# Attention two batches ahead of the output layer, with two float32 batches, in an attention and feed-forward kernel

## The chip, the core and the metric

The kernel runs on one core of a Trainium2 chip. The metric is device time in microseconds of one launch, as a median of several runs. Its engines: TensorE (PE) multiplies matrices and writes the accumulator (PSUM), VectorE (DVE) and ScalarE (ACT) work on elements, GpSimd (POOL) does small work in SBUF, and SyncE (SP) issues the transfers (DMA). Each engine takes its own instructions in order; semaphores order them against each other.

## The reference

```python
scores = (q @ k.T) / sqrt(64) - log(448)          # q, k, v: 8 batches, 12 heads, 448 x 64, float32
attn = 1 / (1 + exp(-scores))                     # a sigmoid, no sum over the row
x = (attn @ v) -> (8 * 448) x 768                 # heads side by side
h = x @ w_in                                      # 768 x 2048
g = where(h > 0, h, exp(min(h, 0)) - 1)           # ELU
out = g @ w_out                                   # 2048 x 768, float32
```

The weights w_in and w_out come as 64-bit floats, the rest as float32.

## The kernel before

**Precision.** A value in float32 is split into a high and a low float16 half (`split`, L120 to L122: ScalarE writes the high half, VectorE the low one), and a product is three matmuls: high x high, low x high, high x low. Scales that are powers of two keep the halves in range. They come from maxima: `magnitude` (L98) multiplies a diagonal by the row maxima (tile `dg`, VectorE), lets TensorE spread it over the partitions (`pb`) and reduces it on VectorE (`al`, then `pw`). Batches below `EXACT` are treated differently: their queries, keys and values stay float32 and go to TensorE as such, each product one float32 matmul instruction or two, so that they need no halves and almost no scales.

**Stages.** A batch has six pairs of heads. For a pair, `prepare` (L294) works in three steps, which callers can place apart: the maxima and `dg`; the scales (`pb`, `al`, `pw`, `sc`, on TensorE, VectorE and GpSimd); and `transposed` (L331), which for a float32 batch transposes queries and keys on TensorE into the accumulator (tile `pt`) and copies them out to `early`, and for the others makes the halves `nat` and transposes them by DMA to `qk` (L352), and makes the halves `vn` of the values. Then a `Pair` computes `scores` (L384, tile `psc`, two buffers) for four groups of keys (three of 128 for both heads, one with the last 64 of each), `soften` (the sigmoid at L395, and for float16 batches the halves `at` at L413 and L414), `values` (L425, L433, tile `pav`, one buffer) and `finish` (`split` to `xh`, and its maximum). Two buffers of `xh` hold the attention of two batches.

After six pairs `rescale` (L443) brings the pairs of a batch to one scale, `moe1` (L479) computes the hidden layer `g` in 16 blocks of 18 matmuls with their exponentials (`ph` at L499, `e` at L511 to L514, `split` to `g`), and `moe2` (L558) computes the output in tiles of 48 matmuls (`po`, L529), which come in 16 steps of three. An even batch has six such tiles (96 steps); an odd one eight (128 steps), as the last 64 tokens of both batches share a tile for each half of the columns.

**Before the loop.** Batch 0 is float32. Beside its pairs, w_in is loaded in 16 tiles (768 KB each) to `stage`, turned from 64-bit floats to magnitudes and signs (`magnitudes`, `signed`, L132 to L159) and split to `wi`; the list `W_IN` says how many tiles are done behind each pair. Then batch 0's hidden layer is computed, and beside it w_out is treated, by a generator of 64 steps (`load_w_out`, L202): for each half of the columns 16 steps that load and turn a block, and 16 that split one. `w_out_beside` makes four steps (`W_OUT`) for each block of the hidden layer from the third on. w_out's tile `wo` shares its place with `stage`. This part is put in order by a planner, which takes the program's order as priority and issues what is ready by its own model of the times.

**The loop** (from L686) runs over batches 1 to 7, and there the order of TensorE, ScalarE, VectorE and SyncE is the program's. Round b mixes the attention of batch b with the output of batch b - 1, then computes the hidden layer of b:

```python
for t in range(2): p.scores(t); p.soften(t)
third()                                  # halves and DMA transpose for the next pair
# loads for the third pair ahead
fill(gap)                                # output steps of three matmuls
second = prepare_pair(n + 2)             # maxima and dg
for t in range(2, NC + 1): p.scores(t); p.soften(t)
fill(share - gap - tail)
third = second()                         # pb, al, scales
for t in range(NC + 1): p.values(t)
p.finish(); fill(tail)                   # tail: four steps in the last pair, 0 in the others
```

In the last pair the generator `hidden` has been started (`next(h)`, the rescaling) ahead of the second `fill`; the second `next(h)` behind the six pairs computes the hidden layer. ScalarE keeps the sigmoid and the exponential in different tables; an order is added so that it changes table once each way for a batch (L398). Lines of the groups below that many parts share: L121 and L122 are `split`, L125 is `absmax`, L105 to L114 are `magnitude`.

## Time and profile before

| | |
|---|---|
| median of 3 runs | 1272.22 us (1271.79 to 1273.72) |
| the profiled execution | 1270.86 us |
| its span | 1269.1 us |
| TensorE busy | 1200.2 us, 95% |
| VectorE busy | 823.4 us, 65% |
| ScalarE busy | 671.8 us, 53% |
| GpSimd busy | 84.1 us, 7% |
| mean granted clock of TensorE | 0.984 |

The profile has one execution. Its span is the time from the first to the last instruction; busy time of TensorE is modelled for the ends of its matmuls, so that back-to-back matmuls overlap a little and the distance of their starts is the better price. A group of instructions is listed by line, engine, operation and tile, with the count, busy time, mean duration of one in ns, and the idle time of its engine just before them with what ended it. The chain of waits is followed back from the last instruction.

### The profile page before, as it was taken

What the parts mean: (1) busy time and instruction counts of PE and PEld (TensorE: products, weight loads), DVE (VectorE), ACT (ScalarE), POOL (GpSimd) and SP (SyncE); (2) the same over time, 40 slices, a digit from 0 to 9 for tenths busy, and PEclk for the clock granted to TensorE, in tenths of its full rate; (3) what the DMA queues carried; (4) which work ended last, traced back from release to release, by engine and by line L of the source; (5) the groups of instructions that cost most, each with busy time, mean ns of one, the idle gap of its engine ahead of it and who ended that gap; (6) DMA issues with size and microseconds to landing.
All of it is one profiled execution on the core that took longest, in us unless ns stands there. A gap on an engine that the chain in (4) does not pass through costs nothing.

```text
span 1269.1 us, 19337 instructions
## 1 busy us (share of the span) xinstructions
PE 1200.2 (95%) x7246; PEld 610.5 (48%) x7246; DVE 823.4 (65%) x1872; ACT 671.8 (53%) x1015; POOL 84.1 (7%) x319
## 2 busy tenths in 40 slices
PE   5979868999999999999999999999999999999998
PEld 2324334445555554545455554545455554455565
DVE  5898989765766557775666646885576656765500
ACT  5867777643655337744555436654565435663400
POOL 0011001100000000010000000010000100100000
PEclk9889979999999999999999999999999999999999
DMA  8937423420233103340144201440034401410000
GB/s 229 281 100 222 126 77 80 100 49 1 60 84 89 37 1 83 89 86 1 37 92 92 50 1 43 105 103 7 1 86 92 92 1 22 106 43 7 1 25 26
DMA packets 213407, 89.76 MB, mean 71 GB/s; under 512 B 177472, under 2 KB 209216, under 8 KB 213312
## 3 DMA queue, kind: packets, MB, share of 16 engines
q1 hardware_dynamic: 213312, 88.51, 28.7%
q8 instruction: 57, 0.93, 0.3%
q14 instruction: 38, 0.31, 0.1%
HBM read 58.20 MB, written 11.01 MB: 55 GB/s over the span
## 4 chain that ended last, share of the span: by engine, by line
PE 78%; ACT 8%; DVE 7%; DMA 3%; issue 2%; SPq 2%; DVEq 0%; POOL 0%; ACTq 0%; POOLq 0%
PE ph L499 31%; PE po L529 25%; PE psc L384 7%; PE pav L433 6%; PE po_r L529 5%; PE pav L425 3%; ACT sg L395 2%; DMA stage<-in_moe_w_in_dram 2%; ACT at L413 1%; SPq L262 1%; PE pb L110 1%; ACT L395 1%; ACT e L511 1%; DVE e L514 1%; DMA so<-in_moe_w_out_dram 1%
## 5 line engine op out<-in xcount | busy, mean ns | idle before, releaser
L499 PE MATMUL ph<-xh,wi 128*128 128x448 f16 x2304 | 442.0, 353 | 6.1 <-DVE xh L122 2.4
L529 PE MATMUL po<-wo,g 128*128 128x384 f16 x2304 | 392.9, 328 | 0.0
L529 PEld LDWEIGHTS <-g 128*128 128x128 f16 x2688 | 257.2, 98 | 198.4 <-issue 36.3
L499 PEld LDWEIGHTS <-wi 128*128 128x128 f16 x2304 | 225.3, 98 | 218.4 <-issue 7.6
L511 ACT ACTIVATE e<-ph,msc 128x448 f32<-128x448 f32 x128 | 80.8, 633 | 211.7 <-PE ph L499 211.6
L414 DVE SCALAR_TENSOR_TENSOR at<-sg,at 128x896 f16<-128x896 f32 x126 | 137.2, 1090 | 84.5 <-ACT at L413 84.5
L395 ACT ACTIVATE sg<-psc,bias,sc 128x896 f32<-128x896 f32 (+1 forms) x168 | 166.6, 992 | 1.7
L513 DVE TENSOR_SCALAR e<-e 128x448 f32<-128x448 f32 x128 | 50.3, 394 | 170.8 <-ACT e L511 170.7
L121 ACT ACTIVATE xh<-pav,sc 128x448 f16<-128x448 f32 x48 | 30.3, 632 | 216.7 <-PE pav L425 216.7
L384 PE MATMUL psc<-qk 64*128 64x448 f16 x1008 | 116.6, 355 | 11.4 <-ACT sg L395 11.4
L413 ACT ACTIVATE at<-sg 128x896 f16<-128x896 f32 x126 | 119.8, 951 | 4.1
L121 ACT ACTIVATE g<-e,msc 128x384 f16<-128x384 f32 (+1 forms) x192 | 96.0, 534 | 6.0 <-DVE e L514 4.3
L122 DVE SCALAR_TENSOR_TENSOR g<-e,msc,g 128x384 f16<-128x384 f32 (+1 forms) x192 | 94.6, 521 | 0.6
L514 DVE SCALAR_TENSOR_TENSOR e<-ph,msc,e 128x448 f32<-128x448 f32 x128 | 87.3, 683 | 4.0
L384 PEld LDWEIGHTS <-qk 64*128 64x128 f16 x1008 | 41.7, 97 | 89.7 <-issue 60.2
L433 PE MATMUL pav<-at,vn 128*64 128x448 f16 x756 | 80.2, 357 | 0.0
L324 POOL TENSOR_SCALAR sc<-pw 128x1 f32<-128x1 f32 x42 | 12.4, 295 | 843.5 <-DVE pw L114 790.9
L529 PE MATMUL po_r<-wo,g 128*128 128x384 f16 x384 | 64.7, 326 | 0.0
L122 DVE SCALAR_TENSOR_TENSOR xh<-pav,sc,xh 128x448 f16<-128x448 f32 x48 | 32.7, 680 | 48.7 <-ACT xh L121 48.7
L433 PEld LDWEIGHTS <-vn 128*64 128x64 f16 x756 | 39.4, 110 | 50.0 <-issue 27.8
L122 DVE SCALAR_TENSOR_TENSOR nat<-raw,sc,nat 128x384 f16<-128x384 f32 (+1 forms) x126 | 59.1, 524 | 0.0
L121 ACT ACTIVATE nat<-raw,sc 128x384 f16<-128x384 f32 (+1 forms) x126 | 58.8, 529 | 0.0
(103 smaller groups left out, 852.7 us busy)
## 6 DMA issues: line engine op xcount, KB each, us to landing
stage<-in_moe_w_in_dram SPq DMA_DIRECT2D x16, 768.0 KB, 6.6
raw<-in_q_dram SPq DMA_DIRECT2D x96, 96.0 KB, 3.1
raw<-in_k_dram SPq DMA_DIRECT2D x96, 96.0 KB, 2.6
rv<-in_v_dram SPq DMA_DIRECT2D x48, 192.0 KB, 2.7
out_dram<-o SPq DMA_DIRECT2D x48, 192.0 KB, 2.1
wo<-in_moe_w_out_dram SPq DMA_DIRECT2D x19, 384.0 KB, 4.1
so<-in_moe_w_out_dram SPq DMA_DIRECT2D x13, 384.0 KB, 4.3
raw<-in_q_dram SPq DMA_DIRECT2D x48, 32.0 KB, 2.4
```

The source lines that it names most:

```text
L121: nc.scalar.mul(hi, src, s)
L122: nc.vector.scalar_tensor_tensor(lo, src, s, hi, op0=ALU.mult, op1=ALU.subtract)
L384: nc.tensor.matmul(psc[:, j, :S] if g < NC else psc[rows[j], 0, :S], kk[rows[j], o], qq[rows[j], :S], start=(n == 0), stop=(n == len(parts ...
L395: a = nc.scalar.activation(sg[:, :nb], psc[:, :nb, :S], AF.Sigmoid, bias=bias, scale=self.s_scale)
L413: nc.scalar.mul(hi, sg, 2.0**ATOP)
L414: nc.vector.scalar_tensor_tensor(lo, sg, 2.0**ATOP, hi, op0=ALU.mult, op1=ALU.subtract)
L433: nc.tensor.matmul(pav[rows[j], :S], vv[i][:, j * NC + g], sg[k][:, j], start=(g == 0 and n == 0), stop=False,)
L499: nc.tensor.matmul(ph[:, :S], wi[:, wj, c, f * P : (f + 1) * P], xh[:, c, xj], start=(n == 0), stop=(n == 3 * NK - 1),)
L511: a = nc.scalar.activation(e, ph[:, :S], AF.Exp, scale=inv)
L513: nc.vector.tensor_scalar(e, e, 1.0, -1.0, op0=ALU.min, op1=ALU.add)
L514: nc.vector.scalar_tensor_tensor(e, ph[:, :S], inv, e, op0=ALU.mult, op1=ALU.max)
L529: nc.tensor.matmul(po[:, :HM], lh(gj, f), wo[:, i, f, wj], start=(n == 0), stop=(n == 3 * NF - 1),)
```

## The change

`EXACT` becomes 2, so batch 1 is computed in float32 too, ahead of the loop. The loop runs over batches 2 to 7; round b mixes the attention of b with the output of b - 2, and then computes the hidden layer of b - 1. Behind the loop come the output of batch 6, the hidden layer of batch 7 and the output of batch 7. The rescaling is cut in five, one piece for each of the first five pairs, and the four reserved steps (`tail`) go. w_in's tiles are spread a little differently over batch 0's pairs. w_out's treatment begins behind the seventh pair: five steps behind each of the pairs 7 to 12, two for each block of batch 0's hidden layer, and the rest in the loop. `prepare_pair(n + 2)` moves behind the last scores of a pair, and its scales (`second()`) move from ahead of the values to behind the next pair's first two groups of scores, straight before the halves; the first pair of a round takes 10 output steps there and no longer 8. In a float32 pair ScalarE copies one half of the transposed queries and keys from the accumulator and VectorE the other. The exponentials of batch 0 are ordered behind the last sigmoid of batch 1, and `xs` has a third buffer.

```diff
-    EXACT = 1
+    EXACT = 2
-    W_IN = [1, 3, 6, 9, 12, 15, 16]
+    W_IN = [1, 3, 6, 9, 12, 14, 16, 16, 16, 16, 16, 16, 16]
+    W_OUT_FROM = 6
-    W_OUT = 4
+    W_OUT, W_OUT_PAIR = 2, 5
...
-                nc.vector.tensor_copy(qk, pt[:, : 2 * S])
+                nc.scalar.copy(qk[:, :S], pt[:, :S])
+                nc.vector.tensor_copy(qk[:, S:], pt[:, S : 2 * S])
...
-            if b - 1 in last_exp:
+            last_sigmoid[b] = a.ins.name
+            if b - EXACT in last_exp:
                 tc.add_manual_dep(
                     a.ins,
-                    last_exp[b - 1],
+                    last_exp[b - EXACT],
...
         for c in range(NP - 1):
             nc.vector.tensor_scalar(xh[:, c], xh[:, c], rr[:, c : c + 1], None, op0=ALU.mult)
+            yield
...
+            if b == 0:
+                tc.add_manual_dep(
+                    a.ins,
+                    last_sigmoid[EXACT - 1],
...
-            xs_of[b] = sb.tile([P, 3, NP], F32, tag="xs", name=f"xs{b}", bufs=2)
+            xs_of[b] = sb.tile([P, 3, NP], F32, tag="xs", name=f"xs{b}", bufs=3)
...
+    def w_out_begin():
+        nonlocal wo, steps
+        w_in_ratios()
+        wo = sb.tile([P, NH, NF, 2, HM], F16, tag="wo", name="wo")
+        steps = load_w_out(wo)
+
     def w_out_beside(f):
-        if f >= 2:
-            step(W_OUT)
-        if f == NF - 1:
-            step(1)
+        step(W_OUT)
...
+        if n == W_OUT_FROM:
+            w_out_begin()
+        if n >= W_OUT_FROM:
+            step(W_OUT_PAIR)
-    third = prepare_pair(EXACT * NP + 1)()
+    second = prepare_pair(EXACT * NP + 1)
...
-            tiles = moe2(b - 1, g, wo)
-            left = NF * NH * (NC + (b - 1) % 2)
+            tiles = moe2(b - 2, g, wo)
+            left = NF * NH * (NC + b % 2)
...
-                tail = 4 if hp == NP - 1 else 0
...
-                third()
+                second()()
...
-                gap = 8 if hp == 0 else 5
+                gap = 10 if hp == 0 else 5
                 fill(gap)
-                second = prepare_pair(n + 2)
                 for t in range(2, NC + 1):
                     p.scores(t)
                     p.soften(t)
+                second = prepare_pair(n + 2)
...
-                if hp == NP - 1:
-                    h = hidden(b)
+                if hp == 0:
+                    h = hidden(b - 1)
+                if hp < NP - 1:
                     next(h)
-                fill(share - gap - tail)
-                third = second()
+                fill(share - gap)
                 for t in range(NC + 1):
                     p.values(t)
                 p.finish()
-                fill(tail)
...
-        out_scale(*of_moe2)
-        for _ in moe2(B - 1, g, wo):
-            pass
+        for b in range(B - 2, B):
+            out_scale(*of_moe2)
+            if b < B - 1:
+                h = hidden(b + 1)
+                for _ in range(NP - 1):
+                    next(h)
+            for _ in moe2(b, g, wo):
+                pass
+            if b < B - 1:
+                of_moe2 = next(h)
```

More of the change, by code (lines that the diff above doesn't have):

```diff
@@ L240, in load_w_out @@
                 yield
-    last_exp = {}
+    last_exp, last_sigmoid = {}, {}
     def load_keys(dst, rest, src, b, h0):
@@ L453, in rescale @@
         )
-        yield
         mx, xp, xr = (rr[:, NP + i : NP + i + 1] for i in range(3))
@@ L512, in moe1 @@
             last_exp[b] = a.ins.name
+            if b == 0:
+                tc.add_manual_dep(
+                    a.ins,
+                    last_sigmoid[EXACT - 1],
+                    mybir.DependencyInfo(
+                        mybir.DependencyClass.NoSync, mybir.DependencyReason.DATA
+                    ),
+                    reason="one change of tables",
+                )
             nc.vector.tensor_scalar(e, e, 1.0, -1.0, op0=ALU.min, op1=ALU.add)
@@ L614, in prepare_pair @@
         return second
-    def w_out_beside(f):
-        nonlocal wo, steps
-        if f == 0:
-            w_in_ratios()
-            wo = sb.tile([P, NH, NF, 2, HM], F16, tag="wo", name="wo")
-            steps = load_w_out(wo)
-        if f >= 2:
-            step(W_OUT)
-        if f == NF - 1:
-            step(1)
+    def w_out_begin():
[3 more added lines that the diff above has]
+        steps = load_w_out(wo)
+    def w_out_beside(f):
+        step(W_OUT)
     def pair_of(n):
@@ L634, in hidden @@
         whole = rescale(b, xh, xs)
-        next(whole)
-        yield
+        for _ in range(NP - 1):
+            next(whole)
+            yield
         xp, xr, rest = next(whole)
@@ L678, in attention_ffn @@
     h = hidden(0, w_out_beside)
-    next(h)
+    for _ in range(NP - 1):
+        next(h)
     of_moe2 = next(h)
@@ L729, in attention_ffn @@
             of_moe2 = next(h)
-        out_scale(*of_moe2)
-        for _ in moe2(B - 1, g, wo):
-            pass
+        for b in range(B - 2, B):
+            out_scale(*of_moe2)
+            if b < B - 1:
+                h = hidden(b + 1)
+                for _ in range(NP - 1):
+                    next(h)
+            for _ in moe2(b, g, wo):
+                pass
+            if b < B - 1:
+                of_moe2 = next(h)
 _INS = ["q", "k", "v", "moe_w_in", "moe_w_out"]
```

## The prediction

> **What bounds the kernel now.** I read the page first, then the chain of waits in order of time, then windows cut at the stages that the chain shows.
>
> ```profile
> span 1269.1 us, 19337 instructions
> PE   5979868999999999999999999999999999999998
> ```
>
> From the sixth slice on TensorE is at 9 tenths nearly everywhere; only the first five slices (159 us) and slice 40 have room. The chain gives the length of a batch, because every run of 270 hidden matmuls is one piece of it:
>
> ```profile
> 269.27 51.09 PE ph L499 x270
> ...
> 421.99 51.09 PE ph L499 x270
> ...
> 563.55 51.09 PE ph L499 x270
> ...
> 716.27 51.09 PE ph L499 x270
> ...
> 1151.20 51.08 PE ph L499 x270
> 1202.28 23.40 PE po L529 x144
> 1225.68 7.80 PE po_r L529 x48
> ...
> 1256.88 7.81 PE po_r L529 x48
> ```
>
> A loop round with 128 output steps (the output of an odd batch) takes 421.99 - 269.27 = 152.72 us, one with 96 steps 563.55 - 421.99 = 141.56. Of these, 51.09 are the run itself, so from the end of a run to the next run's start a 96-step round takes 90.47. A hidden matmul costs 51.09/270 = 0.189 us, an output matmul 23.40/144 = 0.1625.
>
> Going back 90.47 from 269.27, the kernel stands as if the hidden layer of batch 0 had ended, with nothing left over, at **178.8 us**. That early stretch is where the change works:
>
> ```profile
> 30.00:87.00 57.00, 47.56 (x232) 17.54 (x233) 51.01 (x130) 46.27 (x60) 4.83 (x13) 0.88 0.75 219
> 87.00:103.00 16.00, 12.86 (x76) 6.68 (x75) 15.14 (x50) 7.81 (x11) 4.95 (x14) 1.00 0.07 17
> 103.00:162.40 59.40, 52.60 (x269) 25.47 (x268) 54.72 (x121) 46.05 (x94) 2.84 (x9) 0.97 0.60 185
> 162.40:178.80 16.40, 6.87 (x38) 3.11 (x36) 10.88 (x22) 11.29 (x20) 0.00 (x0) 0.77 0.31 96
> ```
>
> Columns: stretch, length, busy time of TensorE, its weight loads, VectorE, ScalarE, GpSimd, then granted clock, DMA share and GB/s. To 103 us the float32 pairs and w_in keep VectorE at 89 to 95%; to 162.4 the hidden layer of batch 0 and w_out keep it at 92%; then TensorE starves (6.87 of 16.40) while w_out is finished. Before 178.8 VectorE is the bound, behind it TensorE.
>
> **The change, part by part.**
>
> *A batch moves from float16 three times to float32 twice.* What one float32 pair costs TensorE is read from start to start in a stretch without gaps:
>
> ```profile
> 58.91 0.97 PE L384 MATMUL psc<-early 64*64 64x448 f32 x4
> 59.81 0.97 PE L433 MATMUL pav<-sg,rv 128*64 128x448 f32 x4
> 60.72 0.98 PE L337 MATMUL pt<-ident,raw 128*128 128x128 f32 x7
> 61.54 0.92 PE L425 MATMUL pav<-sg,rv 128*128 128x448 f32 x2
> 62.38 1.02 PE L384 MATMUL psc<-early 64*128 64x448 f32 x4
> ```
>
> A scores group takes 0.90, a values group 0.91, the seven transposes 0.82, the rest of the values 0.84: 4 x 0.90 + 3 x 0.91 + 0.82 + 0.84 = 8.0 us a pair, 48 for six. What the batch cost in the loop is read from a 96-step round:
>
> ```profile
> 473.08:563.55 90.47, 85.56 (x578) 43.00 (x579) 68.25 (x156) 57.03 (x76) 8.95 (x37) 1.00 0.42 91
> ```
>
> 90.47 less 288 output matmuls (46.8) and the first 18 hidden ones (3.4) leaves 40.3, of which TensorE stood 90.47 - 85.56 = 4.9: 35.4 of work. So TensorE has 12.6 us more to do, and the change can pay only by filling idle time.
>
> *The early stretch anew.* From 87 us TensorE has 48 (six pairs), 288 x 0.189 = 54.5 (hidden layer of batch 0), 32 sums of w_out at 0.1625 = 5.2 and about 1 for the maxima: **109 us**. VectorE has the rows above, 15.14 + 54.72 + 10.88 = 80.7, and for each new pair:
>
> ```profile
> L125 DVE TENSOR_REDUCE mx<-rv 128x1 f32<-128x512 f32 x48 | 32.6, 679 | 0.6 <-DMA rv<-in_v_dram 0.5 <-issue 0.2
> ...
> L122 DVE SCALAR_TENSOR_TENSOR xh<-pav,sc,xh 128x448 f16<-128x448 f32 x48 | 32.7, 680 | 48.7 <-ACT xh L121 48.7
> ...
> L125 DVE TENSOR_REDUCE xs<-xh 128x1 f32<-128x448 f16 x48 | 29.2, 609 | 0.0
> ...
> L341 DVE COPY early<-pt 128x896 f32<-128x896 f32 x6 | 6.5, 1090 | 8.2 <-PE pt L337 8.0
> ...
> L122 DVE SCALAR_TENSOR_TENSOR wo<-wo,swo 128x384 f16<-128x384 f32 x28 | 16.4, 613 | 2.6 <-ACT wo L121 2.3
> ...
> L395 ACT ACTIVATE sg<-psc,bias 128x896 f32<-128x896 f32 (+1 forms) x24 | 21.0, 906 | 2.1 <-PE psc L384 2.1
> ```
>
> 0.68 + 0.68 + 0.61 + half of 1.09 + some 0.5 of small ones = 3.0, six times 18; about 10 more splits of w_out before the loop (the steps left over at 178.8) 6; less half a copy for each of the first six pairs, 3.3: 101 us. ScalarE: 7.81 + 46.05 + 11.29 = 65, four sigmoids a pair (21.0/6 = 3.5), the split of xh and the new half copy at about 0.6 each (estimate, from the 0.68 and half of 1.09 on VectorE): 28, splits 6, three or four for the first six pairs: 102. TensorE is the longest. How closely it can be filled is the one number that I choose: 1.00 as the upper bound, 47.56/57 = 0.83 (the first six pairs beside w_in) as the lower. 103 to 162.4 gave 52.60/59.40 = 0.89 with VectorE as the bound; here w_out's steps lie beside 109 us of matmuls, not beside 60, and VectorE needs 101 of the time, so I take 0.90: 121 us, so the hidden layer of batch 0 ends at **208 us** (196 to 218), against 178.8.
>
> The stretch from 162.4 had the clock at 0.77 while TensorE stood. [...]
>
> *Attention two batches ahead.* Hidden layer b-1 no longer waits for the last pair of b, so its four reserved output steps go back before the values. The wait that this shortage of cover made goes too:
>
> ```profile
> PE pb L110 <- DVE dg L105: 11.6, 6, 2.0
> ...
> ACT xh L121 <- PE pav L425: 216.7, 41, 7.4
> ```
>
> ```profile
> 486.75 0.32 PE L110 MATMUL pb<-dg,ones 128*128 128x384 bf16 x1 [1.97 <-DVE dg L105]
> ...
> 555.05 0.32 PE L110 MATMUL pb<-dg,ones 128*128 128x384 bf16 x1 [1.91 <-DVE dg L105]
> ```
>
> Six such waits of 1.9 us: one in the first and one in the last pair of each of three 96-step rounds. Those of the last pairs go: 1.9 in each. In the first pair the wait for dg goes, but the chain below takes its place, and the gap of 10 steps for 8 only moves filling from one wait to the other: zero for both. The five rescalings (0.45 each) now lie one to a pair beside output matmuls; their cover is a VectorE that is 75% busy there (68.25 of 90.47); without it each would delay the pair by its 0.45.
>
> *Scales move behind the next pair's first scores.* This is the edit that can cost. Now they are ready when ScalarE reaches the split of nat:
>
> ```profile
> 508.17 1.40 ACT L121 ACTIVATE nat<-raw,sc 128x384 f16<-128x384 f32 x3
> 508.30 1.09 DVE L414 SCALAR_TENSOR_TENSOR at<-sg,at 128x896 f16<-128x896 f32 x1 [0.88 <-ACT at L413]
> ...
> 510.78 1.54 SPq L352 DMA_TRANSPOSE qk<-nat  x1
> 511.09 0.95 ACT L413 ACTIVATE at<-sg 128x896 f16<-128x896 f32 x1
> ...
> 514.32 1.89 PE L433 MATMUL pav<-at,vn 128*64 128x448 f16 x18
> ...
> 515.46 0.55 DVE L112 TENSOR_REDUCE al<-pb 128x3 f32<-128x384 f32 x1
> ...
> 516.93 0.23 POOL L319 TENSOR_SCALAR sc<-sc 128x3 f32<-128x3 f32 x1
> ...
> 517.09 1.12 PE L384 MATMUL psc<-qk 64*128 64x448 f16 x10
> ```
>
> and of the transposes of all pairs
>
> ```profile
> DMA to landing us min/median/max: 3.9/4.0/5.5
> ```
>
> After the change al stands behind the second low half (ends 509.39), and al to the scales takes 517.16 - 515.46 = 1.7, so nat begins near 511.1, not 508.17: 2.9 later. Behind nat on ScalarE stand the split of vn and the last two sigmoids, and for them wait the values: the third high half ends at 512.04 + 2.9 = 515.0, its low half 1.09 later at 516.1, where the last two values want it at about 515.9. VectorE's part of nat ends some 2.6 later, so the transpose is issued at 513.4 and lands 4.0 later at 517.4, where the next scores started at 517.09. So the pair grows by about **0.3 us**. On SP the loads of the third pair ahead stand behind the waiting transpose, with two pairs to spare. Bounds: 0 (it is all within the slack) and 1.0 (VectorE's work for a pair and its waits for POOL and ScalarE in a row). In a 128-step round the pair has over 2 us more output matmuls, and the cost is zero. Three 96-step rounds x (5 x 0.3 + 0.2 for the first pair) = 5 us (0 to 15).
>
> *Nothing:* the third xs buffer, the other split of w_in's tiles, the added order behind the last sigmoid (the exponentials wait for the last pair's values anyway).
>
> **The sum.** To the next run of hidden matmuls: 208 + 90.47 - 1.9 = 296.6. Then three rounds of 152.72 and two of 139.66: 737.5. Then the run itself 51.09, the output of batch 6 46.8, the hidden layer of batch 7 54.5, the output of batch 7 23.40 + 7.80 + 23.40 + 7.81 = 62.4, and the 4.4 from 1264.69 to the end: 219.2. With the 5 of the scales: **1258.3 us** of span. The profiled execution took 1270.86 for its span of 1269.1, and the median is 1272.22; with these 3.1 I say **1261 us**.
>
> **The rivals.**
>
> *Slower: the second float32 batch keeps the pace of the first.* Place: pairs 7 to 12.
>
> ```profile
> L425 PE MATMUL pav<-sg,rv x12: 539/540/643, 25.3 to 87.0; 128*128 128x448 f32 x12
> ```
>
> Six pairs from 25.3 to 87.0 are 12.3 us a pair, though TensorE needs 8.0: ScalarE, VectorE and TensorE pass one pair back and forth, with w_in's tiles queued in between. For it: w_out's five steps a pair (each about 1.1 us of VectorE and of ScalarE while it loads, 0.6 while it splits) queue in the same places. Against: in that stretch w_in also kept the DMA engines at 0.75. Price: 6 x 12.3 = 74, then 57 us of hidden layer and sums at 0.89, 64: 225, and 1278 us. It decides from (221 - 87 - 64)/6 = 11.7 us a pair, where the sum passes 1274.8.
>
> *No change: the chain of the scales costs its upper bound.* 15 pairs x 1.0 in place of 5: 1271 us. For it: VectorE's queue in a pair, whose order is now fixed through two other engines. Against: ScalarE stood idle 216.7 us in 41 waits for the values before the split of xh (the row above), 5.3 each, more than the 2.9 that is added.
>
> *Faster still: TensorE is filled throughout.* It ends at 196 to 198, 1250 us. Against: VectorE would be over 92% busy.
>
> **How the numbers follow.** Forecast 0.50 (1254 to 1269, which is the early stretch ending at 201 to 216), filled throughout 0.12, scales 0.14, slow pairs 0.24. A change within 0.2% (2.5 us) can't be told from none here. Faster 0.62, same 0.15, slower 0.23. The range reaches from the filled stage to the slow pairs: 1249 to 1279.
>
> **What would show it.** The hidden layer of batch 0 ends near 208 us; the run of 270 matmuls that follows the first loop round starts near 297; rounds of 152.7 and about 141. Waits of TensorE for dg at the ends of batches are gone. Wrong if the float32 pairs after 87 us are over 11.7 us apart, or if the 96-step rounds are over 144 us.

## The result and the profile after

The changed kernel takes a median of 1287.76 us (1287.18 to 1288.71), the kernel before 1272.15 us in the same runs: the ratio is 1.0121 (95% interval 1.0103 to 1.0139). The change makes it 1.2% slower. The forecast was 1261 us in a range of 1249 to 1279, so the sign is wrong and the time lies outside the range.

The page of the changed kernel begins as follows (span, then TensorE's busy tenths and the granted clock in 40 slices of 32 us):

```profile
span 1285.8 us, 19086 instructions
PE   5778899899999999999999999999999999999998
PEclk9879999999999999999999999999999999999999
```

Slice 6 (159 to 190 us), in which TensorE starved before, is full now (9 for 6), as forecast; a smaller hole, slice 8, lies behind the hidden layer of batch 0 in its new place. But slice 2 is emptier than before (7 for 9), and the clock is at 8 and 7 tenths in slices 2 and 3, which is the first float32 batch.

Next the chain of waits in order of time (start, length, engine, work). Each run of 270 hidden matmuls ends a stage, as before:

```profile
321.66 51.09 PE ph L502 x270
...
474.60 51.09 PE ph L502 x270
...
617.76 51.09 PE ph L502 x270
...
770.69 51.09 PE ph L502 x270
...
913.69 51.09 PE ph L502 x270
...
1066.48 51.08 PE ph L502 x270
```

And windows of the changed kernel, cut where the last values of the sixth and of the twelfth float32 pair start and where the hidden layer of batch 0 ends (stretch, length, busy time of TensorE, weight loads, VectorE, ScalarE, GpSimd, clock, DMA share, GB/s):

```profile
30.00:60.00 30.00, 19.97 (x108) 7.73 (x108) 21.11 (x53) 23.27 (x33) 0.92 (x5) 0.94 0.91 268
60.00:100.40 40.40, 33.25 (x151) 12.13 (x152) 31.98 (x81) 27.58 (x35) 2.90 (x11) 0.75 0.47 123
100.40:168.60 68.20, 57.97 (x251) 18.48 (x250) 54.59 (x150) 55.14 (x95) 5.41 (x18) 0.97 0.54 162
168.60:227.10 58.50, 56.80 (x303) 28.51 (x302) 45.39 (x96) 33.34 (x62) 3.44 (x9) 1.00 0.33 95
```

The forecast, stage by stage, against these rows:

| stage | forecast, us | measured, us |
|---|---|---|
| sixth float32 pair | 87 (as before, 86.6) | 100.4 |
| from there to the end of batch 0's hidden layer | 121 | 227.1 - 100.4 = 126.7 |
| from there to the next run of 270 | 88.6 and 1.7 for the scales | 321.66 - 227.1 = 94.6 |
| 128-step rounds | 152.72 | 152.94, 152.93, 152.79 |
| 96-step rounds | 139.66 and 1.7 | 143.16, 143.00 |
| the rest | 219.2 | 1285.8 - 1066.48 = 219.3 |

The span is 27.5 us over the forecast's 1258.3. The first batch brings 13.4 of it, the second batch and the hidden layer 5.7, the first round 4.3, the two 96-step rounds 3.4; the remaining 0.7 is spread over the rest. So 19 of 27.5 us were lost before the loop begins, and half of the whole in the first batch, in which the change touches only the copy in halves and the place of one tile of w_in.

### The profile page after: what moved, and what is told of

The parts are those of the page before. It is cut to its first block, busy times and chain, and to the rows that moved or that the text cites. A ratio compares the mean times of both kernels' runs of the same rounds, so it can differ in the third digit from the quotient of the medians.

```text
span 1285.8 us, 19086 instructions
## 1 busy us (share of the span) xinstructions
PE 1221.2 (95%) x7204; PEld 616.5 (48%) x7204; DVE 789.9 (61%) x1794; ACT 648.3 (50%) x983; POOL 85.0 (7%) x289
## 4 chain that ended last, share of the span: by engine, by line
PE 65%; ACT 13%; DVE 11%; DMA 5%; issue 4%; SPq 1%; POOL 0%; DVEq 0%; ACTq 0%; POOLq 0%
PE ph L502 30%; PE po L541 19%; PE po_r L541 5%; ACT sg L397 4%; PE psc L386 4%; PE pav L436 4%; ACT at L416 3%; DMA stage<-in_moe_w_in_dram 2%; PE pav L428 2%; DVE at L417 2%; DVE mt L126 1%; ACT nat L122 1%; DMA so<-in_moe_w_out_dram 1%; DVE wo L123 1%; DVE mx L126 1%
## 5 line engine op out<-in xcount | busy, mean ns | idle before, releaser
L541 PE MATMUL po<-wo,g 128*128 128x384 f16 x2304 | 387.0, 326 | 0.4 <-DVE e L526 0.4
L417 DVE SCALAR_TENSOR_TENSOR at<-sg,at 128x896 f16<-128x896 f32 x108 | 117.8, 1091 | 90.7 <-ACT at L416 90.3
L397 ACT ACTIVATE sg<-psc,bias,sc 128x896 f32<-128x896 f32 (+1 forms) x144 | 142.7, 991 | 2.9 <-PE psc L386 1.2
L416 ACT ACTIVATE at<-sg 128x896 f16<-128x896 f32 x108 | 102.6, 950 | 3.4
L386 PE MATMUL psc<-qk 64*128 64x448 f16 (+1 forms) x864 | 100.2, 356 | 1.4 <-ACT sg L397 0.8
L122 ACT ACTIVATE nat<-raw,sc 128x384 f16<-128x384 f32 (+1 forms) x108 | 50.9, 533 | 100.2 <-POOL sc L320 100.2
L123 DVE SCALAR_TENSOR_TENSOR g<-e,msc,g 128x384 f16<-128x384 f32 (+1 forms) x192 | 94.6, 521 | 2.8 <-ACT g L122 2.4
L436 PE MATMUL pav<-at,vn 128*64 128x448 f16 x648 | 73.5, 358 | 14.3 <-ACT at L416 10.7
L549 DVE TENSOR_SCALAR o<-po,osc 128x384 f32<-128x384 f32 x48 | 29.4, 613 | 78.8 <-PE po L541 71.6
L386 PEld LDWEIGHTS <-qk 64*128 64x128 f16 (+1 forms) x864 | 35.4, 98 | 70.0 <-issue 39.7
L386 PE MATMUL psc<-early 64*128 64x448 f32 (+1 forms) x192 | 54.4, 651 | 7.2 <-DVE early L343 2.9
```

Source lines behind the costliest of these rows:

```text
L122: nc.scalar.mul(hi, src, s)
L123: nc.vector.scalar_tensor_tensor(lo, src, s, hi, op0=ALU.mult, op1=ALU.subtract)
L386: nc.tensor.matmul(psc[:, j, :S] if g < NC else psc[rows[j], 0, :S], kk[rows[j], o], qq[rows[j], :S], start=(n == 0), stop=(n == len(parts ...
L397: a = nc.scalar.activation(sg[:, :nb], psc[:, :nb, :S], AF.Sigmoid, bias=bias, scale=self.s_scale)
L416: nc.scalar.mul(hi, sg, 2.0**ATOP)
L417: nc.vector.scalar_tensor_tensor(lo, sg, 2.0**ATOP, hi, op0=ALU.mult, op1=ALU.subtract)
```

## The experiments

All stage times come from the traces: "sixth" and "twelfth" are the starts of the last values matmuls of those float32 pairs, "hidden 0" is the start of the last matmul of batch 0's hidden layer, "round" is the first 96-step round between two runs of 270. The "first round" in the text goes from the end of batch 0's hidden layer to the end of the next run of 270. The ratio is against the kernel before.

A trace is one execution. In the six kernels with one copy on VectorE (those named with one_copy) the traces have the same order of instructions on every engine up to the sixth pair, and yet it stands anywhere between 86.2 and 90.9 us. So a difference of less than 5 us in that column is not shown by two traces.

| kernel | sixth | twelfth | hidden 0 | round | median, us | ratio (95%) |
|---|---|---|---|---|---|---|
| before | 86.6 | - | 161.8 | 141.6 | 1272.2 | 1 |
| after | 100.4 | 168.6 | 226.9 | 143.2 | 1287.8 | 1.0121 (1.0103 to 1.0139) |
| after_one_copy | 90.4 | 158.9 | 218.1 | 143.3 | 1276.8 | 1.0027 (1.0011 to 1.0042) |
| before_two_copies | 99.8 | - | 170.2 | 141.5 | 1279.5 | 1.0044 (1.0031 to 1.0058) |
| after_copies_vector | 94.1 | 159.4 | 216.9 | 144.4 | 1279.0 | 1.0045 (1.0031 to 1.006) |
| after_copy_scalar | 90.8 | 155.8 | 212.6 | 143.3 | 1273.6 | 1.0005 (0.9992 to 1.0019) |
| before_copy_scalar | 88.6 | - | 168.2 | 141.5 | 1275.0 | 1.0015 (1.0001 to 1.0028) |
| after_w_in | 100.6 | 175.3 | 233.1 | 143.6 | 1294.3 | 1.0161 (1.0144 to 1.0178) |
| after_scales | 99.4 | 173.3 | 236.2 | 141.2 | 1288.8 | 1.0119 (1.0098 to 1.014) |
| before_moved_scales | 85.9 | - | 164.4 | 146.8 | 1291.6 | 1.0149 (1.0128 to 1.0171) |
| one_copy_scales | 86.4 | 155.8 | 221.0 | 141.2 | 1274.2 | 1.0016 (0.9999 to 1.0032) |
| one_copy_scales_w33 | 86.2 | 153.7 | 218.3 | 141.2 | 1273.1 | 1.0009 (0.9995 to 1.0024) |
| one_copy_late | 86.4 | 147.4 | 216.5 | 143.7 | 1285.6 | 1.011 (1.0092 to 1.0129) |
| one_copy_scales_loop | 90.9 | 158.5 | 217.1 | 141.2 | 1269.6 | 0.9982 (0.9969 to 0.9995) |
| one_copy_scales_loop_w62 | 89.4 | 157.4 | 218.4 | 141.2 | 1268.0 | 0.9973 (0.9958 to 0.9988) |
| copy_scalar_scales | 90.8 | 156.9 | 214.6 | 141.1 | 1268.3 | 0.996 (0.9947 to 0.9973) |
| copy_scalar_scales_w62 | 90.2 | 154.6 | 213.3 | 141.3 | 1267.4 | 0.9953 (0.9936 to 0.997) |

### The copy in halves

**The changed kernel with one copy.**

```diff
-                nc.scalar.copy(qk[:, :S], pt[:, :S])
-                nc.vector.tensor_copy(qk[:, S:], pt[:, S : 2 * S])
+                nc.vector.tensor_copy(qk, pt[:, : 2 * S])
```

> The changed kernel with one edit undone: VectorE alone copies queries and keys out of the accumulator. In the changed kernel the first six float32 pairs end at 100.4 us instead of 86.6 (the start of the last values matmul of the sixth pair), and the stage before the loop ends at 227 instead of the 208 forecast. Theory A (the half copy on ScalarE holds them up, since scores now wait for whichever of two queues is later): the sixth pair is back near 87 to 90 us and the kernel 10 to 14 us shorter, about 1275. Theory B (the copy is not the cause; twelve float32 pairs and w_out put the planned part in another order): within 4 us of 1287.8, sixth pair near 100.

Measured: the sixth pair at 90.4 instead of 100.4, 11.0 us of the median gone.

**The kernel before with two copies**: the same edit the other way round.

> The kernel before with that one edit alone: one half of queries and keys copied by ScalarE, the other by VectorE. Theory A: the sixth float32 pair comes 8 to 14 us later than 86.6 us, and the kernel takes about 1280 us. Theory B: within 3 us of 1272.2.

Measured: the sixth pair at 99.8 instead of 86.6. The hidden layer of batch 0 takes back a part (it ends 8.4 us later), and the median is 6.8 us above the 1272.7 of the kernel before in the same runs. This edit, for which no wait was costed, is worth 7 us here and 11 there. In the four traces with halves in two queues (after, before_two_copies, after_w_in and after_scales) the sixth pair stands at 99.4 to 100.6 us, in the twelve with a whole copy at 85.9 to 90.9.

How it works is seen in the timeline of before with two copies, at the end of its second pair (start, length, engine, line, instruction):

```profile
41.00 0.98 PE L337 MATMUL pt<-ident,raw 128*128 128x128 f32 x7
...
42.04 0.56 ACT L341 COPY early<-pt 128x448 f32<-128x448 f32 x1
...
43.03 0.95 DVE L157 SCALAR_TENSOR_TENSOR stage<-stage 128x768 uint32<-128x768 uint32 x1
...
43.46 1.02 PE L385 MATMUL psc<-early 64*128 64x448 f32 x4
...
43.90 0.62 DVE L342 COPY early<-pt 128x448 f32<-128x448 f32 x1
...
44.86 1.02 PE L385 MATMUL psc<-early 64*128 64x448 f32 x4
```

The transposes are done near 42.0 and ScalarE's half starts at once, at 42.04. VectorE's half starts at 43.90: ahead of it in VectorE's queue stands a 0.95 us instruction for a tile of w_in. The next scores, at 43.46, start before that half does. They don't read it: a pair is transposed ahead of the scores of the pair before it, so the transposes are the fourth pair's and the scores the third's. What the scores need is room in the accumulator. `pt`, which the transposes write, is one of the two buffers of `psc` (`tag="psc", bufs=2` in the kernel), and it comes free when both halves are copied out. The first group of scores takes the other buffer; the second starts at 44.86, 0.34 us behind the end of VectorE's half (43.90 + 0.62 = 44.52).

It is so throughout. In the changed kernel's trace the first group behind the transposes starts before the last copy ends in eleven of twelve pairs; the second never does, and in eight pairs it starts within 0.25 us of that end. So the later of two queues sets when the scores go on, and w_in's tiles stand in both. From the end of the transposes to the end of the last copy it is, as a mean of the first six pairs, 3.2 us here and 1.2 in the kernel before; 3.6 in the changed kernel, 1.4 with one copy on VectorE, 1.7 with one on ScalarE and 1.6 with both halves on VectorE.

What TensorE waited for in the first batch, from 20 us to the sixth pair's end, for the kernel before:

```profile
PE pav L433 <- ACT sg L395: 7.1, 3, 3.6
PE psc L384 <- ACT sg L395: 2.9, 4, 1.5
20.00:87.50 67.50, 54.25 (x274) 20.58 (x273) 61.31 (x158) 54.69 (x71) 5.61 (x18) 0.90 0.80 226
```

for before with two copies:

```profile
PE pav L434 <- ACT sg L396: 15.7, 6, 4.9
20.00:100.80 80.80, 59.01 (x290) 22.90 (x287) 64.64 (x165) 59.17 (x79) 5.87 (x18) 0.85 0.69 190
```

(waited for: total, times, longest; the last row is the window). TensorE's idle time rises from 67.50 - 54.25 = 13.3 us to 21.8. The wait that grows is for the sigmoid, which is late because its scores are late; the scores themselves hardly show a wait for a copy, since TensorE is given other work there. That is 8.5 of the 13.3 us by which this stretch is longer. The rest is slower work: TensorE is busy 4.8 us longer, for 16 instructions more, at a clock of 0.85 instead of 0.90. Windows in the loop, below, show the clock at 0.50 behind some waits.

**Which property of the halves it is.** In one kernel both halves are on VectorE, in another one whole copy is on ScalarE:

```diff
-                nc.scalar.copy(qk[:, :S], pt[:, :S])
+                nc.vector.tensor_copy(qk[:, :S], pt[:, :S])
```

> The changed kernel with both half copies on VectorE, as two instructions. Theory A1 (ScalarE is the cause: in the first batch its queue holds w_in's work, and its half of the copy comes late): the sixth pair is near 87 to 91 us as with one copy, and the kernel takes 1274 to 1280. Theory A2 (two instructions instead of one change the planner's order, whichever engine runs them): the sixth pair near 100, about 1287.

```diff
-                nc.scalar.copy(qk[:, :S], pt[:, :S])
-                nc.vector.tensor_copy(qk[:, S:], pt[:, S : 2 * S])
+                nc.scalar.copy(qk, pt[:, : 2 * S])
```

> The changed kernel with the whole copy on ScalarE, as one instruction. Theory A1: the sixth pair near 100 us or later, 1285 to 1295. Theory A2: near 87 to 91 us and about 1277. Theory A3 (what hurts is that the scores wait for the later of two queues): like A2, since there is one queue again.

Measured: 94.1 us with two halves in one queue, 90.8 with one copy on ScalarE, 90.4 with one on VectorE, 100.4 with halves in both queues. The theory that ScalarE's queue is the wrong place fell: the whole copy on ScalarE gives the lowest median of the four, 1273.6 us, though its interval overlaps that of one copy on VectorE; VectorE is relieved of 12 x 1.09 = 13 us there, and the second batch takes 65.0 us instead of the 68.5 with one copy on VectorE. Two queues instead of one are worth 8.8 us of the median (1287.8 for 1279.0) with the same two instructions. Whether two instructions in one queue cost anything is not shown: the medians are 2.2 us apart (1279.0 and 1276.8) and the intervals overlap. On ScalarE the whole copy takes 0.90 us, from the groups of that kernel:

```profile
L342 ACT COPY early<-pt 128x896 f32<-128x896 f32 x12 | 10.8, 900 | 5.7 <-PE pt L338 5.7
```

**The kernel before with its copy on ScalarE**: the same edit.

> The kernel before with the whole copy of queries and keys moved to ScalarE. Theory A3 (it is the split over two queues that costs): the sixth pair within 4 us of 86.6 and the kernel within 4 us of 1272.6, where the two halves on two engines cost 7 us. Theory A2 in its strict form (any change of the copy reorders the early stretch for the worse): 1276 or more. If ScalarE is simply the better place for it: 1265 to 1269.

Measured: 1.0015 (1.0001 to 1.0028), 2.3 us slower by the medians. So in the kernel before, with six float32 pairs, the copy on ScalarE brings nothing.

### The scales behind the next pair's scores

**The kernel before with the scales moved**, alone:

```diff
-    third = prepare_pair(EXACT * NP + 1)()
+    second = prepare_pair(EXACT * NP + 1)
...
-                third()
+                second()()
...
-                second = prepare_pair(n + 2)
                 for t in range(2, NC + 1):
                     p.scores(t)
                     p.soften(t)
+                second = prepare_pair(n + 2)
...
-                third = second()
```

> The kernel before with the move of maxima and scales alone. Theory: a pair in the rounds with 96 output steps grows from 13.66 to 13.93 us, the wait for dg in the first pair turns into a wait of the values of about 3 us that halves the clock for one 3.4 us stretch (1.4 us), the wait for dg in the last pair goes (1.9): those rounds end up 141 to 143 us against 141.56, rounds with 128 steps stay at 152.7, and the kernel is within 0 to 5 us of 1272.7. Rival (the move costs nothing by itself): rounds at 139.7 and the kernel 4 to 6 us faster.

Measured: 1.5% or 19.0 us slower, where 0 to 5 was expected. The three 96-step rounds between runs take 146.8, 146.5 and 142.1 us instead of 141.6, 143.2 and 139.1, the 128-step rounds 153.4 instead of 152.7, and 7.7 us are lost ahead of the first run of 270 (not taken apart here). Waits in the first of these rounds, from ahead of the values of its first pair to the next run of hidden matmuls, of the kernel before:

```profile
PE pb L110 <- DVE dg L105: 3.9, 2, 2.0
```

and with the scales moved:

```profile
ACT nat L121 <- POOL sc L319: 16.8, 6, 2.9
...
PE pav L433 <- ACT at L413: 2.9, 2, 1.6
PE pav L433 <- DVE at L414: 1.3, 3, 0.6
```

The wait of nat for the scales is there, 16.8/6 = 2.8 us a pair, as the prediction worked it out (2.9). TensorE now waits for the halves `at` of the third group (high at L413, low at L414) in the first and in the last pair of the round. These waits cost more than they last. Windows of 3.4 us each, during and after the wait of the first and of the last pair:

```profile
493.90:497.30 3.40, 1.21 (x12) 0.53 (x8) 2.18 (x4) 2.65 (x4) 0.00 (x0) 1.00 0.57 110
497.30:500.70 3.40, 3.40 (x12) 1.09 (x12) 3.27 (x10) 0.67 (x2) 0.00 (x0) 0.50 0.58 126
...
565.60:569.00 3.40, 1.59 (x14) 0.69 (x10) 2.18 (x4) 2.52 (x3) 0.00 (x0) 1.00 0.61 116
569.00:572.40 3.40, 3.40 (x10) 1.52 (x9) 3.23 (x12) 0.63 (x1) 0.00 (x0) 0.50 0.59 131
```

After 3.40 us in which TensorE was busy for only 1.21 or 1.59, the clock is at 0.50 for the next 3.40; half of that, 1.7 us, is the estimate of what is lost in each. Two such stretches make 3.4 of the 5.2 us of this round. All waits of TensorE in it come to 5.9 us instead of 3.9, which is about the rest.

**The changed kernel with the scales where they were**, those of pair 13 ahead of the loop:

```diff
-    second = prepare_pair(EXACT * NP + 1)
+    third = prepare_pair(EXACT * NP + 1)()
...
-                second()()
+                third()
...
+                second = prepare_pair(n + 2)
                 for t in range(2, NC + 1):
                     p.scores(t)
                     p.soften(t)
-                second = prepare_pair(n + 2)
...
                 fill(share - gap)
+                third = second()
```

> The changed kernel with the maxima and the scales placed as before (maxima ahead of a pair's third group of scores, scales ahead of its values, halves behind the next pair's second group). If the moved scales are what lengthens the rounds with 96 output steps from 139.7 (141.6 less the wait of the last pair) to 143.1 us, those rounds come to 139 to 141.6 and the kernel is 5 to 9 us shorter, about 1280. If their cost is a wait that only changes its name, they stay at 143 and the time within 2 us. Rival: the wait for dg in the first and last pair comes back, 3.8 us a round, and the gain is half.

Measured: the rounds fall to 141.2 as expected, and the total stays (1.0119 for 1.0121) where about 1280 us was expected. What the rounds win from the first run of 270 to the end of the loop, 5.5 us, is lost in front of it, 7.9: the scales of pair 13, now ahead of batch 0's hidden layer, and another order of w_out's work make pairs 7 to 12 take (173.3 - 99.4)/6 = 12.3 us each and let the hidden layer end 9 us later (these two causes are not parted). So the moved scales cost nearly 2 us in each 96-step round of the changed kernel, and there is a better place for the first of them.

**One copy on VectorE and the edit above** (one_copy_scales):

> The changed kernel with the copy by VectorE alone and the scales placed as before. If the two losses are separate and add up: rounds with 96 output steps 141.2 us as in the run with the old scales, the sixth pair near 90 and the hidden layer of batch 0 at its end near 218 us as in the run with one copy, about 1271 us, no different from the kernel before. If the planner's order of the early stretch changes with any edit of the loop, the end of the hidden layer lies up to 8 us elsewhere and the total with it.

**The same with the scales of pair 13 inside the loop's first pair** (one_copy_scales_loop). Ahead of the loop it stays as changed; inside it differs from the edit above by this:

```diff
-                third()
+                if n == EXACT * NP:
+                    third = second()
+                third()
```

> The changed kernel with the copy by VectorE alone and the scales placed as before inside the loop, but the scales of the second pair of batch 2 still inside the loop and not ahead of batch 0's hidden layer. With them ahead, that hidden layer took 67.5 us (153.5 to 221.0) and not 62.7. If that is what gave the early stretch 3 us back, it ends near 218 and the rounds with 96 output steps take 141.2: 1268 to 1272 us. Rival: the planner's order shifts anyway, 1272 to 1278.

Measured: with pair 13's scales ahead of the hidden layer 1274.2 us, inside the loop 1269.6, against 1276.8 with one copy alone. The second is the first version whose interval lies below the kernel before (0.9982, 0.9969 to 0.9995). Its instructions ahead of the loop come in the same order as with one copy alone, so the 7.2 us between these two medians come from the scales' place in the loop. The placement inside the loop keeps hidden 0 at 217 and has the short rounds too.

### w_in and w_out beside the second batch

**The old split of w_in's tiles** (the sixth entry 15 instead of 14):

```diff
-    W_IN = [1, 3, 6, 9, 12, 14, 16, 16, 16, 16, 16, 16, 16]
+    W_IN = [1, 3, 6, 9, 12, 15, 16, 16, 16, 16, 16, 16, 16]
```

> The changed kernel with w_in's tiles spread as before (15 done behind the fifth pair, not 14). Theory A and theory B: no difference beyond 2 us of 1287.8. If the spread of w_in is what slows the first six pairs, the sixth ends near 90 us and the kernel takes about 1277.

Measured: 6.6 us slower than the changed kernel, where no difference was expected. The sixth pair stays (100.6), the pairs behind it take 12.5 us each. This window goes from the sixth to the twelfth pair in that kernel, to be held against the row 100.40 to 168.60 above:

```profile
100.60:175.30 74.70, 61.61 (x253) 20.07 (x250) 56.42 (x149) 55.55 (x96) 5.46 (x18) 0.91 0.47 145
```

Nearly the same number of matmuls (253 and 251) takes 3.6 us more at a clock of 0.91 for 0.97, and TensorE stands 2.9 us longer. An edit costed at nothing is worth 6 us: it doesn't change how much work there is, only which tile stands ahead of which pair and, with it, the order of the queues.

**w_out's work behind the twelfth pair instead of the seventh**, with one copy:

```diff
-    W_OUT_FROM = 6
+    W_OUT_FROM = 11
-    W_OUT, W_OUT_PAIR = 2, 5
+    W_OUT, W_OUT_PAIR = 4, 1
```

> The changed kernel with the copy by VectorE alone and w_out taken away from the float32 pairs: it begins behind the twelfth pair with one step, and batch 0's hidden layer has four steps a block, as before. With w_out beside them the pairs 7 to 12 are 11.4 us apart (90.4 to 158.9), and the hidden layer of batch 0 ends at 218.3. Theory C (w_out's steps in ScalarE's and VectorE's queues set that pace): the pairs come 8 to 9.5 us apart, the twelfth near 143 us, and the hidden layer takes 66 to 75 us in place of 62, so that the total changes by less than 8 us. Theory D (a float32 pair is a chain through three engines that is no faster without w_out): 10.5 us or more apart, and the kernel is 8 to 20 us longer than 1276.8.

Measured: pairs 7 to 12 take (147.4 - 86.4)/6 = 10.2 us in place of 11.4, so w_out's steps cost them 1.2 us each; 10.2 lies between the two theories. That the rest above TensorE's 8.0 is the chain through the engines is argued, not shown. But the hidden layer of batch 0 takes 73.6 us in place of 62.7 and the first round 152.8 in place of 145.9, and the total is 8.8 us above one copy alone. Windows over the hidden layer of batch 0, of this kernel:

```profile
142.90:216.50 73.60, 65.28 (x337) 32.12 (x335) 61.39 (x132) 47.18 (x90) 2.76 (x10) 0.98 0.42 121
```

and of the changed kernel with one copy:

```profile
155.40:218.10 62.70, 61.14 (x324) 30.39 (x323) 50.19 (x107) 37.52 (x70) 6.05 (x15) 1.00 0.32 92
```

VectorE's work moves (61.39 for 50.19), TensorE stands 8.3 us instead of 1.6. Beginning w_out early is a part of the change that pays.

**Other shares of w_out**: three steps beside each hidden step and three a pair; and, in the version with the scales in the loop, six a pair instead of five.

```diff
-    W_OUT, W_OUT_PAIR = 2, 5
+    W_OUT, W_OUT_PAIR = 3, 3
```

> As the run before this in the list, with three steps of w_out behind each of the pairs 7 to 12 and three for each block of the hidden layer (five and two in the changed kernel), so that w_out is done before the loop. If w_out's steps slow the pairs (theory C): pairs 7 to 12 near 10 us apart, the hidden layer 62 to 66 us, and the first loop round 3 to 4 us shorter since nothing of w_out is left over: 1262 to 1268 us, faster than both kernels. If not (theory D): no difference beyond 4 us from 1271.

```diff
-    W_OUT, W_OUT_PAIR = 2, 5
+    W_OUT, W_OUT_PAIR = 2, 6
```

> As the run before this in the list, with six steps of w_out behind each of the pairs 7 to 12 in place of five, so that all 64 are made before the loop. If what is left of w_out lengthens the first loop round (142.7 to 146 us against 141.2), it falls to 141.2 to 142 while the pairs grow by up to 1 us each: no difference beyond 3 us. A version faster than both kernels would need the pairs to stay at 11.4 us: 1265 to 1268.

Measured: 1273.1 against 1274.2, and 1268.0 against 1269.6. Both differences are smaller than the intervals. In the trace of the second the first round is 143.4 us long instead of 146.5; no step of w_out is left over for it, where two were.

### The parts that paid, together

The whole copy on ScalarE and the scales as in one_copy_scales_loop; then six steps of w_out a pair (W_OUT_PAIR = 6) as well:

> The changed kernel with the whole copy on ScalarE and the scales placed as before inside the loop. If the gains of the two runs add up (hidden layer of batch 0 at its end at 212.6 in place of 226.9; rounds with 96 output steps 141.2 in place of 143.1): 1264 to 1269 us, faster than both kernels, and what is left of the forecast's 1261 is that the early stretch ends 5 us later than 208 and the first round is 3 us long. Rival (the planner's order shifts again): 1269 to 1276.

> As the run before this in the list with six steps of w_out behind each of the pairs 7 to 12, so that none is left for the loop. With the copy by VectorE this made 1.7 us: 1262 to 1268 if it adds up. Rival (ScalarE, which now has the copy too, is what the pairs wait for): pairs 7 to 12 over 11.5 us apart and 1268 to 1272.

Measured: 1268.3 us and 1267.4 us, ratios 0.996 (0.9947 to 0.9973) and 0.9953 (0.9936 to 0.997). The latter is 20 us below the changed kernel and has the lowest median of all. Its windows, from 30 us to the sixth pair, to the twelfth and to the end of batch 0's hidden layer:

```profile
30.00:90.20 60.20, 46.98 (x259) 18.51 (x259) 48.96 (x125) 52.45 (x67) 5.86 (x16) 0.94 0.76 217
90.20:154.60 64.40, 55.28 (x252) 18.87 (x250) 53.10 (x143) 54.69 (x92) 2.88 (x11) 1.00 0.59 171
154.60:213.30 58.70, 56.87 (x302) 28.41 (x301) 49.37 (x108) 39.05 (x72) 3.95 (x15) 1.00 0.34 95
```

The first batch ends 10 us earlier than in the changed kernel, the second takes 64.4 instead of 68.2 us with the clock at 1.00, and hidden 0 stands at 213.3, in the forecast's bounds of 196 to 218.

## Why the prediction was wrong

**The step that failed first: "the new half copy at about 0.6 each", and the 87 us that the early stretch started from.** The sum took the time of the first batch from the trace of before and began with "from 87 us". The half copy was costed in engine time alone: 0.55 us of VectorE less, 0.6 of ScalarE more, each pair. The engine times were nearly right:

```profile
L343 DVE COPY early<-pt 128x448 f32<-128x448 f32 x12 | 7.4, 614 | 1.4 <-ACT early L342 1.4
L342 ACT COPY early<-pt 128x448 f32<-128x448 f32 x12 | 6.3, 528 | 11.4 <-PE pt L338 11.4
```

(groups of the changed kernel: 0.61 and 0.53). What was missed is that the buffer of the accumulator, which the next scores need, then comes free only with the later of two copies, in two queues in which w_in's work stands. For the moved scales the prediction had asked what is queued around each wait; it did not ask it of the copy, since it saw only a shorter instruction on each engine. With one copy the same batch ends at 90.4, and the time is 11.0 us lower. The two halves on two engines measured 1287.8 us and both on VectorE 1279.0, the whole on one engine 1273.6 and 1276.8. So in this kernel the measurement decides against halves on two engines.

**From the sixth pair to the end of batch 0's hidden layer: right in its mechanism, 5.7 us too short.** Forecast were 109 us of TensorE's work, filled at 0.90. The same stretch in the changed kernel and, below it, in the version with the whole copy on ScalarE:

```profile
100.40:227.10 126.70, 114.76 (x552) 46.99 (x551) 99.97 (x244) 88.48 (x156) 8.85 (x26) 0.99 0.44 131
```

```profile
90.80:212.60 121.80, 112.03 (x552) 47.32 (x550) 99.63 (x242) 89.96 (x157) 8.02 (x26) 1.00 0.47 136
```

The filling is 114.76/126.70 = 0.906: the number that the prediction chose. VectorE's 100 us are the 101 that it counted; ScalarE's are 88 in place of 102. The term that was too small is TensorE's, 114.8 for 109: w_out's sums take 7.2 us for the 5.2 of the sum, the six pairs 49.8 for 48, and 1.3 go to scores of the loop's first pair, which the sum did not count here. In the second row the stretch takes 121.8 us where 121 was forecast. So the forecast's 208 for the end of the hidden layer would have come out within some 5 us, had the first batch kept its time.

**The rival that came closest, and why it isn't the cause.** "The second float32 batch keeps the pace of the first" gave 225 us for the early stretch; 227.1 were measured. But its mechanism, pairs over 11.7 us apart, did not decide. The last values of the float32 pairs behind the first batch, one row of the changed kernel:

```profile
L428 PE MATMUL pav<-sg,rv x16: 539/539/643, 90.7 to 168.9; 128*128 128x448 f32 x16
```

From the sixth pair (100.4) to the twelfth (168.6) it is 68.2/6 = 11.4 us a pair, under the threshold, and the hidden layer behind them took 58.5 of the 64 us that the rival gave it. The largest part of the excess (13.4 of 27.5 us) lies in the first batch, which no rival touched. The total of the rival (1278) is below the measured 1287.6 of the profiled execution.

**The first round: 94.6 us instead of about 90.** The prediction let the first round begin "with nothing left over". Steps of w_out were left, and TensorE waited in the round's first pair. Timeline of the changed kernel:

```profile
237.95 1.32 PE L436 MATMUL pav<-at,vn 128*64 128x448 f16 x12
244.24 0.96 PE L436 MATMUL pav<-at,vn 128*64 128x448 f16 x4 [4.97 <-ACT at L416]
```

This is 5.0 us, where the same place of the next 96-step round has 2.6 (below). The chain of the moved scales is in it, and in its queues stand splits of w_out: two on VectorE, 1.14 us from 238.10, come between `al` and the scales. Six steps of w_out a pair, which leave none over, shorten the round by 3 us in one pair of traces (one_copy_scales_loop and its w62 version) and by 1.4 in the other (copy_scalar_scales and its own). How the 4.3 us divide between w_out and the scales is not shown.

**The 96-step rounds: "zero for both" was wrong, the 0.3 us a pair right.** The last pairs' wait for dg is gone as forecast (the six waits of before belong to four rounds, 1, 2, 2 and 1, and not two to each of three, which changes nothing here). The pairs grew by what was forecast too: the values of the third and fourth pair of a round of the changed kernel start as follows:

```profile
569.00 2.04 PE L436 MATMUL pav<-at,vn 128*64 128x448 f16 x18
582.95 2.03 PE L436 MATMUL pav<-at,vn 128*64 128x448 f16 x18
```

They are 13.95 us apart, and in the chain of the kernel before 13.66 (500.73, 514.39, 528.05): 0.29. And nat waits 100.2 us in 36 times for the scales, 2.8 each where 2.9 was worked out:

```profile
L122 ACT ACTIVATE nat<-raw,sc 128x384 f16<-128x384 f32 (+1 forms) x108 | 50.9, 533 | 100.2 <-POOL sc L320 100.2
```

Wrong was the first pair of the round. For it the prediction said that the chain below takes the place of the wait for dg, "zero for both". The chain is longer than the wait was, and behind it the clock is at 0.51 for 3.40 us:

```profile
540.26 0.57 PE L436 MATMUL pav<-at,vn 128*64 128x448 f16 x4 [2.56 <-ACT at L416]
541.39 0.58 PE L436 MATMUL pav<-at,vn 128*64 128x448 f16 x2 [0.56 <-DVE at L417]
541.90 1.86 PE L428 MATMUL pav<-sg,vr 128*128 128x448 f32 x2
```

```profile
537.60:541.00 3.40, 0.68 (x6) 0.24 (x4) 2.19 (x4) 3.19 (x5) 0.24 (x1) 1.00 0.39 75
541.00:544.40 3.40, 3.01 (x8) 0.91 (x9) 3.23 (x11) 0.59 (x1) 0.00 (x0) 0.51 0.68 141
```

The waits are 3.1 us instead of the 1.97 of before, and behind them 3.0 us of matmuls run at a clock of 0.51 (about 1.5 lost, an estimate: half of 3.0). Together 2.6, less what the pair had in hand: the rounds came out 1.6 to 1.8 over the forecast's 141.4. With the old place of the scales they take 141.2 (after_scales), and not the 139.66 that the forecast began with: there the first pair's wait for dg is still present, is 2.9 us long, and behind it, in the chain, the 18 values matmuls from 547.06 take 3.30 us where those from 562.36 take 1.82.

That the clock was put at nothing in these rounds is a fault of the baseline as well. The forecast took 141.56 us from one round, in which the clock stood at 1.00 (421.99 to 563.55). In the same trace the next 96-step round takes 859.42 - 716.27 = 143.15 us, as long as the changed kernel's; its waits for dg are the same, and behind one of them the clock is at 0.50 (last section). The prediction's reading of the tenths is off in the same way: TensorE stands at 9 from the eighth slice on, and the sixth and seventh (6 and 8) are the ones with room.

**"Nothing" for the split of w_in's tiles was wrong.** Putting the old split back costs 6.6 us. No wait had been seen in it; what changed is the order of the queues.

**What held:** 128-step rounds within 0.22 us, everything from the last run of the loop on within 0.1, the hidden layer of batch 0 (58.5 us for its 57 of work), the end of the waits for dg in the last pairs, and that the gain can only come from filling (TensorE is busy for 1221.2 us in the changed kernel and for 1200.2 in the kernel before). The gain is there, though small: with the whole copy on ScalarE, the scales back in the loop and six steps of w_out a pair, 1267.4 us, which is 0.47% below the kernel before where 0.9% was forecast.

**What stays open.** The halves change two things at once: when the accumulator's buffer comes free, and the order in which the planner issues everything else, which from about 20 us on differs on TensorE, ScalarE and VectorE. The runs don't part them; both follow from the same edit.

## What to carry to other kernels

Here an instruction split over two engines made what needed the buffer that it empties wait for the later of two queues (8.8 us of the median with the same two instructions): cost a split by what stands ahead of each half, not by the shorter halves. An edit "that only moves work" in a stretch where several engines are 80 to 90% busy can't be costed at nothing; give it a price of both signs (here 7 to 11 us for the copy, 6 for a tile of w_in), and take no stage over from the old trace if any instruction in it changed. Test the parts of a change one by one: as a whole this one lost 1.2%, with one copy and the scales back in the loop it won 0.2%, and with that copy on ScalarE and one more step of w_out a pair 0.5%.

## What the runs showed of the hardware

Waits of TensorE of the same length were followed by a half-rate stretch in one place and not in another. In the windows above, stretches of 3.40 us with 1.21 and 1.59 us of matmuls (before_moved_scales) and 0.68 (the changed kernel) were each followed by one at 0.50 or 0.51. In the kernel before, the first pair of a 96-step round waits 1.97 us for dg each time. In the round that begins at 421.99 (wait from 484.78 to 486.75) the clock stays at 1.00; in the one that begins at 716.27 (wait from 779.05 to 781.02) it falls to 0.50:

```profile
481.94:485.35 3.41, 2.83 (x18) 1.57 (x17) 3.41 (x7) 3.37 (x5) 0.00 (x0) 1.00 0.20 41
485.35:488.76 3.41, 2.02 (x19) 0.93 (x18) 3.24 (x11) 0.00 (x0) 0.00 (x0) 1.00 0.79 160
...
781.02 0.32 PE L110 MATMUL pb<-dg,ones 128*128 128x384 bf16 x1 [1.97 <-DVE dg L105]
...
778.90:782.31 3.41, 1.44 (x14) 0.66 (x14) 3.28 (x9) 0.72 (x2) 0.00 (x0) 1.00 0.88 174
782.31:785.72 3.41, 3.41 (x14) 1.03 (x12) 1.37 (x7) 0.01 (x1) 1.12 (x5) 0.50 0.57 128
```

These windows lie on a grid that the two traces of the kernel before and of the changed kernel give: in each, all half-rate stretches begin whole multiples of 3.413 us apart (in the changed kernel those of the loop at 244.04, 541.00 and 837.96 us, 87 steps from one to the next). On this grid the second wait lies within one window, with 1.44 us of matmuls; the first is cut by an edge at 485.35 and leaves 2.83 and 2.02, and so is that of the last such round (1074.93 to 1076.90, edge at 1075.86, 2.48 and 2.37), in which the clock stays at 1.00 as well. These three waits don't show a rule: the window from 92.82 to 96.23 us of the same trace has 1.45 us of matmuls, and the clock behind it stays at 1.00. The round from 716.27, with a half-rate stretch, takes 143.15 us, which is 1.6 us longer than the one from 421.99 without; half of the 3.41 us, 1.7, would be the estimate.

One copy of 128x896 float32 out of the accumulator took 0.90 us on ScalarE (after_copy_scalar) and 1.09 on VectorE (before); in the changed kernel one of 128x448 took 0.53 on ScalarE and one 0.61 on VectorE.
